# Softmax sums and V products of four heads in four 32-column tiles, with V split in even and odd values

## The chip, the cores and the metric

The kernel runs on one core of a Trainium2 chip. Its time is the device time of one execution in microseconds (us). The median of 13 runs before the change is 294.19 us, with runs from 291.63 to 298.27. One execution was profiled; it took 292.19 us, and its span from the first to the last instruction is 290.5 us. Engines are called PE (matrix multiplication), DVE (vector engine), ACT (activations), POOL (general purpose) and SP (issues most DMAs).

## The reference

Attention with forget gates, then a gated convolution FFN:

```python
scores = q @ k.T / sqrt(64)                # 8 batches, 8 heads, 576 positions, 64 values
cum = cumsum(log(clip(f, 1e-4, 1)))
attn = softmax(scores + cum[:, None] - cum[None, :], causal)
x = (attn @ v), the heads side by side     # (8, 576, 512)
h = relu(x @ w_in)                         # 1024 channels
out = (h * sigmoid(conv3(h))) @ w_out      # convolution over positions, per channel
```

The softmax's division is done after the product with V: the kernel computes the sums of the exponentials in a matmul with ones, their reciprocals, and multiplies the V product by them.

## The kernel before

**Tiling.** The 64 pairs of batch and head are worked off in 16 half batches of four heads (`hb`). A half batch consists of two steps (`i = 2*hb + p`) of two heads each (`s`). Scores are computed transposed, keys in partitions and queries along the free axis, in key blocks of 128, and only where the causal mask leaves something: the diagonal blocks (L350), the blocks off the diagonal (L341), and the last 64 positions of all four heads as a "tail" (L327). ACT takes exponentials out of PSUM (L332, L347, L357), POOL masks the diagonal blocks and the tails (L335, L360). The exponentials of a step lie in one of six tiles `pp` (off-diagonal, then masked diagonal), the tails in `pt`.

**Sums and V products.** `sweep` (L368) goes over ten pieces of queries and keys (L363). For every piece it issues one matmul for each of the two heads of the step, head `s` into the partitions `64*s` to `64*s + 63` of PSUM. With ones as weights it makes the sums (`sums`, L384), with V as weights the product (`pv`, L398). A sweep is 20 matmuls of 64 weight columns. The ones of step `c` of a batch stand in column `c` of each 32 columns (L256), so the sums of a batch's four steps are accumulated into different rows of one PSUM tile. `recip` (L389) then transposes this tile in blocks of 32 x 32 (st), and takes the reciprocals of four columns of each block (rt). `spread` (L394), once per step, spreads them over 64 partitions per head with another transpose (rb), and `norm` (L403) multiplies the V product by them and writes xt, the FFN's input. V is loaded for a whole batch and cast to fp16 by POOL, in two instructions per half batch (L231).

**FFN.** For each of eight blocks of 128 channels, `ffn1` (L410, eight matmuls) needs all four xt of the batch. ACT applies ReLU (ht, L418), DVE two steps of the convolution (u, L424 and L426), ACT the tanh (hg, L429) and DVE the gate (L433). `ffn2` (L435) multiplies by w_out; ACT evacuates (L465) and SP stores (L473).

**Order.** The kernel is written as tasks, each with its engine, an assumed duration, the tasks it comes after, the buffers it takes and gives, and a key for its priority. `Plan.play` (L36) runs through these assumed durations when the kernel is built, and fixes in which order each engine gets its instructions. On the chip, every engine works its instructions off in this order and waits where something isn't there yet. SP's and POOL's DMA issues stand in these orders as well. Buffers are rings: four PSUM tiles (ps), four of q and k (qk), six pp, four ht, three u, two each of rb, xt and hg.

**Loading q and k.** q and k arrive by transposing DMAs (L199) as 16-bit halves. In the first six half batches DVE then clears the odd rows (`clamp`, L203, four per half batch), and SP fills in rows of the cumulated gates out of an image in DRAM (`rows_of`, L218, the issues L220 and L221). Later half batches get all these rows by DMA (`fill`, L212). POOL writes the image's constants early on (L479), partly out of the q/k tile of half batch 3, whose load waits for that.

Of the kernel before, what the change touches and what calls it, by code (L numbers as in the profile page):

```python
# [9 lines left out]
FP32 = mybir.dt.float32  # L10
FP16 = mybir.dt.float16
# [103 lines left out]
def kernel(  # L115
# [11 lines left out]
    nc = tc.nc  # L127

    B, H, S, D = q.shape
    assert (B, H, S, D) == (8, 8, 576, 64)  # L130
    NKB = 5
    SL = S - 128 * (NKB - 1)
# [7 lines left out]
    HH = 4  # L140
# [3 lines left out]
    AB = 256  # L144
# [24 lines left out]
    ones_h = cpool.tile([128, 4, 64], FP16, name="ones_h")  # L169
# [5 lines left out]
    va_t = [cpool.tile([128, HH, NKB, 64], FP16, name=f"va{t}") for t in range(NVA)]  # L175
# [5 lines left out]
    rt_t = [cpool.tile([128, 18, 4], FP32, name=f"rt{t}") for t in range(2)]  # L181
# [10 lines left out]
    plan = Plan({"ps": 4, "sc": 2, "mm": 2, "pv": 2, "p": NP, "pt": NPT, "pd": 2, "p3": 2, "st": 1, "rt": 2, "rb": 2, "xt": 2, "ht": NHT,  # L192
                 "u": NU, "hg": 2, "ob": NOB, "va": NVA, "vf": NVF, "qk": RING})
    slot = plan.slot
# [36 lines left out]
    def cast_v(t_load, t_cast, hb, part, eng):  # L231
        vf, va = vf_t[slot[t_load, "vf"]][:, HH * (hb % 2):HH * (hb % 2 + 1)], va_t[slot[t_cast, "va"]]
        if part == 0:
            eng.tensor_copy(va[:, :, 0:4, :], vf[:, :, 0:4, :])  # L234
        else:
            eng.tensor_copy(va[0:SL, :, 4, :], vf[0:SL, :, 4, :])
# [16 lines left out]
    nc.gpsimd.memset(ones_h, 0.0)  # L253
    for c in range(4):
        for j in range(2):
            nc.gpsimd.memset(ones_h[:, c, 32 * j + c:32 * j + c + 1], 1.0)  # L256
# [3 lines left out]
    for t in range(NVA):  # L260
        nc.gpsimd.memset(va_t[t][64:128, :, NKB - 1, :], 0.0)
# [106 lines left out]
    def sweep(ps, i, pp, pt, left_of, first, last):  # L368

        for x, (m, q0, n, kind) in enumerate(PIECES):  # L370
            for s in range(2):
                h = (2 * i + s) % HH
                if kind == "o":
                    c = 1024 * s + OFF[m] + q0 - 128 * (m + 1)
                    p = pp[:, c:c + n]
                elif kind == "d":
                    c = 2048 + 512 * s + 128 * m
                    p = pp[:, c:c + n]
                else:
                    p = pt[:, SL * h:SL * (h + 1)]  # L380
                nc.tensor.matmul(ps[64 * s:64 * (s + 1), AB + q0:AB + q0 + n], left_of(s, h, m), p,  # L381
                                 start=first and x in (0, 3), stop=last and x in (2, 9), skip_group_check=True)

    def sums(t_first, i, t_dg, t_tail):  # L384
        c = i % 4
        sweep(ps_t[slot[t_first, "ps"]], i, pp_t[slot[t_dg, "p"]], pt_t[slot[t_tail, "pt"]],
              lambda s, h, m: ones_h[:, c, :], c == 0, c == 3)

    def recip(t_first, me):  # L389
        st, rt = st_t[0], rt_t[slot[me, "rt"]]  # L390
        nc.vector.transpose(st, ps_t[slot[t_first, "ps"]][:, AB:AB + S])
        nc.vector.reciprocal(rt, st.rearrange("p (b t) -> p b t", t=32)[:, :, 0:4])

    def spread(t_rc, me, c):  # L394
        nc.vector.transpose(rb_t[slot[me, "rb"]].rearrange("p (b t) -> p b t", t=32),  # L395
                            rt_t[slot[t_rc, "rt"]][:, :, c:c + 1].broadcast_to((128, 18, 32)))

    def pv(me, i, t_dg, t_tail, t_va):  # L398
        va = va_t[slot[t_va, "va"]]
        sweep(ps_t[slot[me, "ps"]], i, pp_t[slot[t_dg, "p"]], pt_t[slot[t_tail, "pt"]],  # L400
              lambda s, h, m: va[:, h, m, :], True, True)

    def norm(t_pv, t_rb, t_x0, c):  # L403
        nc.vector.tensor_tensor(xt_t[slot[t_x0, "xt"]][:, c, :], ps_t[slot[t_pv, "ps"]][:, AB:AB + S],  # L404
                                rb_t[slot[t_rb, "rb"]], op=ALU.mult)
# [81 lines left out]
    add = plan.add  # L487
# [21 lines left out]
    for hb in range(NHB):  # L509
# [10 lines left out]
        if hb % 2 == 0:  # L520
            t_vl[b] = add({"SP": 3.4}, [], 4 * b + 2.4, lambda me, b=b: load_v(b, me), take=["vf"], lag=3.0, dma=5.2)
        x = add({"POOL": 1.25}, [t_vl[b]], 4 * b + 3.0 + 0.4 * (hb % 2),
                lambda me, hb=hb, b=b: cast_v(t_vl[b], me, hb, 0, nc.gpsimd), take=["va"])
        y = add({"POOL": 0.5}, [t_vl[b]], 4 * b + 3.1 + 0.4 * (hb % 2),
                lambda me, hb=hb, b=b, x=x: cast_v(t_vl[b], x, hb, 1, nc.gpsimd),
                give=[("vf", t_vl[b])] if hb % 2 else [], behind=[x])
        t_va[hb] = (x, y)
# [36 lines left out]
        if hb == 1:  # L564
            t_win = weights(4, w_in_f16, moe_w_in.rearrange("(cc p) ff -> p cc ff", p=128),
                            [t_mask[1], t_mask[1], t_mask[2], t_mask[2]], 2.2, 256)
# [3 lines left out]
        if hb % 2 == 0:  # L570
            continue
        prev = None
        for c in range(4):
            i = 4 * b + c
            g = i // 2
            need = [t_mask[i], t_tmask[g], t_exp[g, i % 2, 0], t_exp[g, i % 2, 1]]
            if c == 0:
                t_s0 = prev = add({"PE": 0.75}, need + [t_mask[i + 2]], i + 3.6,
                                  lambda me, i=i, g=g: sums(me, i, t_dg[i], t_tail[g]), take=["ps"])
            else:  # L580
                prev = add({"PE": 0.75}, need, 4 * b + 3.6 + 0.1 * c,
                           lambda me, i=i, g=g, t_s0=t_s0: sums(t_s0, i, t_dg[i], t_tail[g]), behind=[prev])
        t_rc = add({"DVE": 1.5}, [prev], 4 * b + 3.5, lambda me, t_s0=t_s0: recip(t_s0, me), take=["rt"],
                   give=[("ps", t_s0)])
        for c in range(4):
            i = 4 * b + c
            g = i // 2
            last = i == 4 * b + 3
            t_rb = add({"DVE": 0.75}, [t_rc], 4 * b + 3.7 + 0.1 * c,
                       lambda me, t_rc=t_rc, c=c: spread(t_rc, me, c), take=["rb"],  # L590
                       give=[("rt", t_rc)] if last else [])
            t_pv[i] = add({"PE": 0.75}, [t_rc, *t_va[g]], 4 * b + 3.8 + 0.1 * c,
                          lambda me, i=i, g=g: pv(me, i, t_dg[i], t_tail[g], t_va[g][0]),
                          take=["ps", "pv"] + (["xt"] if c == 0 else []), behind=[t_pv[i - 1]] if c else [],
                          give=[("p", t_dg[i])] + ([("pt", t_tail[g]), ("va", t_va[g][0])] if c % 2 else []))
            t_norm[i] = add({"DVE": 0.75}, [t_pv[i], t_rb], 4 * b + 3.6 + 0.1 * c,
                            lambda me, i=i, t_rb=t_rb, b=b, c=c: norm(t_pv[i], t_rb, t_x0[b], c),
                            give=[("ps", t_pv[i]), ("pv", t_pv[i]), ("rb", t_rb)],
                            behind=[t_norm[i - 1]] if c else [])
            if c == 0:  # L600
                t_x0[b] = t_pv[i]

    for b in range(B):
        k1 = 4 * b + 5.0
        us = {}
        for ff in range(NFF):
            key = k1 + 0.5 * ff
            x = add({"PE": 1.0}, [t_norm[4 * b + c] for c in range(4)] + [t_win[ff // 2]], key,
# [86 lines left out]
```

## Time and profile before

| what | value |
|---|---|
| median of 13 runs (lowest, highest) | 294.19 us (291.63, 298.27) |
| the profiled execution, its span | 292.19 us, 290.5 us |
| PE busy | 243.1 us (84%) |
| DVE busy | 238.7 us (82%) |
| ACT busy | 197.8 us (68%) |
| POOL busy | 95.7 us (33%) |
| sums and V products (L381), matmuls | 640 and 640 |
| transposes to spread reciprocals (L395) | 32, mean 746 ns |
| products with reciprocals (L404) | 32, mean 729 ns |
| mean granted PE clock | 0.973 |

Busy time is a share of the whole span, which has a head (loads and the first scores), a stretch in which the batches follow each other with nearly the same pattern, and a tail of FFN work alone. A row of the timeline has its start, its length, the engine, the line, the operation with its tiles, and in brackets how long the engine was idle before it and what ended that. Rows can merge several equal instructions (x18). In the chain that ended last, each row is followed back from the last instruction to what released it.

### The profile page before, as it was taken

Reading aid. Unit: us, or ns where it says so; the run is one execution under the profiler, and the core shown is the slowest. Engines: PE = TensorE matmul, PEld = TensorE weight load, DVE = VectorE, ACT = ScalarE, POOL = GpSimd, SP = SyncE. Lnnn points to the kernel's source line nnn. Section 1 sums busy time; section 2 is a strip of 40 time slices with the busy share of each in tenths; the row PEclk is TensorE's granted clock in tenths of the full one; section 3 lists DMA queues with packets and bytes.
Section 4 is the critical chain, followed back from the end, with each engine's and each line's share of the span. In section 5 each row is a group of like instructions: output and inputs, shape, how many; then the busy total and the mean of one; then the engine's idle time right before and its main releaser. Section 6 shows DMA issues by size and latency. Waiting matters only on the chain.

```text
span 290.5 us, 6856 instructions
## 1 busy us (share of the span) xinstructions
PE 243.1 (84%) x2832; PEld 169.7 (58%) x2832; DVE 238.7 (82%) x322; ACT 197.8 (68%) x266; POOL 95.7 (33%) x133
## 2 busy tenths in 40 slices
PE   0099349498789799999998999999999999969990
PEld 0077237376655577567755875687568766854630
DVE  4853209989999888997997899989998999799871
ACT  1238425487665998885868878977897798526731
POOL 8626816236350326405255261126112221000000
PEclk9999958979999999999999999999999999999998
DMA  8997999999987997999999999999411001200404
GB/s 166 227 258 134 159 168 192 173 214 190 233 183 103 289 224 166 259 248 261 187 228 206 271 210 172 222 294 154 108 74 74 20 2 72 93 2 0 165 0 164
DMA packets 125683, 47.71 MB, mean 164 GB/s; under 512 B 117470, under 2 KB 120542, under 8 KB 124992
## 3 DMA queue, kind: packets, MB, share of 16 engines
q1 hardware_dynamic: 118852, 43.73, 72.4%
q0 software_dynamic: 6640, 3.25, 8.3%
q8 instruction: 22, 0.36, 0.6%
q10 hardware_dynamic: 160, 0.30, 0.4%
q14 instruction: 9, 0.07, 0.1%
HBM read 19.91 MB, written 10.58 MB: 105 GB/s over the span
## 4 chain that ended last, share of the span: by engine, by line
PE 46%; DVE 30%; ACT 8%; issue 6%; DMA 4%; POOL 3%; SPq 1%; ACTq 0%; DVEq 0%; POOLq 0%
PE ps L440 14%; PE ps L414 11%; PE ps L381 8%; PE ps L320 6%; DVE u L426 6%; DVE hg L433 6%; DVE u L424 5%; DVE xt L404 4%; DVE rb L395 3%; DMA qk<-image 3%; PE ps L454 3%; ACT pd L357 2%; ACT pp L347 2%; ACT hg L429 2%; DMA rb<-in_f_dram 2%
## 5 line engine op out<-in xcount | busy, mean ns | idle before, releaser
L320 PE MATMUL ps<-qk 128*128 128x128 bf16 (+3 forms) x576 | 63.7, 249 | 30.9 <-DVE qk L205 14.5
L414 PE MATMUL ps<-xt,w_in_f 128*128 128x288 f16 x512 | 72.2, 288 | 4.3 <-DVE xt L404 2.6
L347 ACT ACTIVATE pp<-ps 128x1024 f16<-128x1024 f32 x64 | 64.7, 1027 | 11.6 <-PE ps L320 10.4
L429 ACT ACTIVATE hg<-u,cw 128x576 f16<-128x576 f32 x64 | 49.4, 779 | 25.7 <-DVE u L426 25.4
L320 PEld LDWEIGHTS <-qk 128*128 128x128 bf16 x576 | 39.6, 102 | 43.3 <-issue 15.1
L360 POOL TENSOR_SCALAR_AFFINE_SELECT pp<-pd 128x1024 f16<-128x1024 f32 x32 | 38.5, 1202 | 73.8 <-ACT pd L357 73.5
L414 PEld LDWEIGHTS <-w_in_f 128*128 128x128 f16 x512 | 48.9, 98 | 22.4 <-issue 6.9
L426 DVE SCALAR_TENSOR_TENSOR u<-ht,cwt,u 128x576 f32<-128x576 f16 x64 | 60.8, 959 | 0.7
L433 DVE SCALAR_TENSOR_TENSOR hg<-hg,ht 128x576 f16<-128x576 f16 x64 | 53.1, 838 | 10.0 <-ACT hg L429 9.8
L424 DVE SCALAR_TENSOR_TENSOR u<-ht,cwt 128x576 f32<-128x576 f16 x64 | 55.3, 877 | 4.5 <-ACT ht L418 4.5
L440 PE MATMUL ps<-w_out_f,hg 128*128 128x512 f16 x224 | 51.5, 379 | 2.5 <-ACT pd L357 1.1
L418 ACT ACTIVATE ht<-ps 128x576 f16<-128x576 f32 x64 | 41.3, 657 | 16.4 <-PE ps L414 14.4
L440 PEld LDWEIGHTS <-hg 128*128 128x128 f16 x224 | 21.6, 98 | 26.5 <-issue 2.3
L357 ACT ACTIVATE pd<-ps 128x1024 f32<-128x1024 f32 x32 | 32.8, 1026 | 5.5 <-PE ps L325 2.4
L381 PE MATMUL ps<-pp,ones_h 128*64 128x128 f16 (+3 forms) x576 | 26.4, 243 | 1.4 <-ACT pp L347 0.8
L381 PEld LDWEIGHTS <-ones_h 128*64 128x64 f16 x640 | 23.1, 112 | 6.3 <-issue 4.6
L381 PE MATMUL ps<-pp,va 128*64 128x128 f16 (+3 forms) x576 | 24.9, 239 | 1.5 <-DVE xt L404 1.2
L335 POOL TENSOR_SCALAR_AFFINE_SELECT pt<-p 128x256 f16<-128x256 f32 x16 | 9.4, 589 | 50.0 <-ACT p L332 50.0
L234 POOL CAST va<-vf 128x1024 f16<-128x1024 f32 x16 | 18.3, 1146 | 22.1 <-DMA vf<-in_v_dram 16.1
L381 PEld LDWEIGHTS <-va 128*64 128x64 f16 x640 | 22.4, 111 | 5.6 <-issue 3.9
L395 DVE STREAM_TRANSPOSE rb<-rt 128x576 f32<-128x576 f32 x32 | 22.7, 746 | 0.0
L404 DVE TENSOR_TENSOR xt<-ps,rb 128x576 f16<-128x576 f32 x32 | 22.2, 729 | 0.0
(75 smaller groups left out, 165.8 us busy)
## 6 DMA issues: line engine op xcount, KB each, us to landing
vf<-in_v_dram SPq DMA_DIRECT2D x32, 256.0 KB, 5.9
out_dram<-ob SPq DMA_DIRECT2D x16, 512.0 KB, 2.8
qk<-blank SPq DMA_DIRECT2D x10, 540.0 KB, 5.5
vf<-in_v_dram SPq DMA_DIRECT2D x8, 128.0 KB, 5.1
w_in_f<-in_moe_w_in_dram POOLq DMA_DIRECT2D x4, 256.0 KB, 5.2
w_out_f<-in_moe_w_out_dram POOLq DMA_DIRECT2D x4, 256.0 KB, 7.1
out_dram<-ob SPq DMA_DIRECT2D x16, 64.0 KB, 3.6
blank<-qk POOLq DMA_DIRECT2D x1, 540.0 KB, 4.7
```

The lines of the kernel that those rows point to most:

```text
L320: nc.tensor.matmul(o, tk[:, h * S + k0:h * S + k0 + 128], tq[:, h * S + q0:h * S + q0 + n], start=True, stop=hb > 0)
L347: nc.scalar.activation(pp_t[slot[t_dg, "p"]][:, 1024 * s:1024 * (s + 1)], ps_t[slot[t_sc, "ps"]], AF.Exp, scale=SCALE)
L357: nc.scalar.activation(pd_t[slot[me, "pd"]], ps_t[slot[t_dg, "ps"]], AF.Exp, scale=SCALE)
L360: nc.gpsimd.affine_select(pp_t[slot[t_dg, "p"]][:, 2048:3072].rearrange("p (m j) -> p m j", j=128), pd_t[slot[t_ex, "pd"]].rearrange("p (m ...
L381: nc.tensor.matmul(ps[64 * s:64 * (s + 1), AB + q0:AB + q0 + n], left_of(s, h, m), p, start=first and x in (0, 3), stop=last and x in (2, ...
L414: nc.tensor.matmul(ps[:, MB + 288 * a:MB + 288 * (a + 1)], w_in_f16[:, cc, 128 * ff:128 * (ff + 1)], xt[:, cc, 288 * a:288 * (a + 1)], sta ...
L418: nc.scalar.activation(ht_t[slot[t_m1, "ht"]][:, 1:1 + S], ps_t[slot[t_m1, "ps"]][:, MB:MB + S], AF.Relu, scale=0.5)
L424: nc.vector.scalar_tensor_tensor(u, ht[:, 0:S], cwt[:, ff, 0:1], ht[:, 1:1 + S], op0=ALU.mult, op1=ALU.add)
L426: nc.vector.scalar_tensor_tensor(u, ht[:, 2:2 + S], cwt[:, ff, 1:2], u, op0=ALU.mult, op1=ALU.add)
L429: nc.scalar.activation(hg_t[slot[t_g0, "hg"]][:, ff, :], u_t[slot[t_u, "u"]], AF.Tanh, scale=cw[:, ff, 1:2])
L433: nc.vector.scalar_tensor_tensor(hv, hv, 1.0, ht_t[slot[t_m1, "ht"]][:, 1:1 + S], op0=ALU.add, op1=ALU.mult)
L440: nc.tensor.matmul(o, hg[:, ff, 128 * c:128 * (c + 1)], w_out_f16[:, ff, :], start=(ff == 0), stop=(ff == NFF - 1))
```

## The change

Sums and V products are made for a half batch's four heads at once. Head `h` takes the PSUM partitions `32*h` to `32*h + 31`, with 32 weight columns per matmul. A sweep is then 40 matmuls. V's 64 values don't fit 32 columns, so V is split in even and odd values when it is cast, and a half batch has one sweep of sums and two of V. The reciprocals are made per half batch: one transpose, the reciprocals of one column of each block, one transpose to spread them. Each of the two V sweeps gives one xt, in which partition `32*h + j` holds value `2*j + e` of head `h`. w_in's rows are loaded in this order, with two DMAs in place of four. The cast of V takes three POOL instructions in place of two. Sums and products no longer wait for the second half batch of a batch, and their tasks have new keys.

```diff
-    ones_h = cpool.tile([128, 4, 64], FP16, name="ones_h")
+    ones_h = cpool.tile([128, 32], FP16, name="ones_h")
...
-    va_t = [cpool.tile([128, HH, NKB, 64], FP16, name=f"va{t}") for t in range(NVA)]
+    va_t = [cpool.tile([128, HH, NKB, 2, 32], FP16, name=f"va{t}") for t in range(NVA)]
...
-    rt_t = [cpool.tile([128, 18, 4], FP32, name=f"rt{t}") for t in range(2)]
+    rt_t = [cpool.tile([128, 18, 1], FP32, name=f"rt{t}") for t in range(2)]
...
-        if part == 0:
-            eng.tensor_copy(va[:, :, 0:4, :], vf[:, :, 0:4, :])
-        else:
-            eng.tensor_copy(va[0:SL, :, 4, :], vf[0:SL, :, 4, :])
+        vf = vf.rearrange("p h m (j e) -> p h m e j", e=2)
+        if part < 2:
+            eng.tensor_copy(va[:, :, 0:4, part, :], vf[:, :, 0:4, part, :])
+        else:
+            eng.tensor_copy(va[0:SL, :, 4, :, :], vf[0:SL, :, 4, :, :])
...
-    def sweep(ps, i, pp, pt, left_of, first, last):
+    def sweep(ps, hb, t_dgs, t_tail, left_of):
+        pt = pt_t[slot[t_tail, "pt"]]
         for x, (m, q0, n, kind) in enumerate(PIECES):
-            for s in range(2):
-                h = (2 * i + s) % HH
+            for h in range(HH):
+                pp, s = pp_t[slot[t_dgs[h // 2], "p"]], h % 2
...
-                nc.tensor.matmul(ps[64 * s:64 * (s + 1), AB + q0:AB + q0 + n], left_of(s, h, m), p,
-                                 start=first and x in (0, 3), stop=last and x in (2, 9), skip_group_check=True)
+                nc.tensor.matmul(ps[32 * h:32 * (h + 1), AB + q0:AB + q0 + n], left_of(h, m), p,
+                                 start=x in (0, 3), stop=x in (2, 9), skip_group_check=True)
...
+    def recip(t_s, me):
+        st, rt, rb = st_t[0], rt_t[slot[me, "rb"]], rb_t[slot[me, "rb"]]
+        nc.vector.transpose(st, ps_t[slot[t_s, "ps"]][:, AB:AB + S])
+        nc.vector.reciprocal(rt, st.rearrange("p (b t) -> p b t", t=32)[:, :, 0:1])
+        nc.vector.transpose(rb.rearrange("p (b t) -> p b t", t=32), rt.broadcast_to((128, 18, 32)))
+
+    def pv(me, hb, e, t_dgs, t_tail, t_va):
         va = va_t[slot[t_va, "va"]]
+        sweep(ps_t[slot[me, "ps"]], hb, t_dgs, t_tail, lambda h, m: va[:, h, m, e, :])
...
         if hb == 1:
-            t_win = weights(4, w_in_f16, moe_w_in.rearrange("(cc p) ff -> p cc ff", p=128),
-                            [t_mask[1], t_mask[1], t_mask[2], t_mask[2]], 2.2, 256)
+            for x in range(2):
+                t_win.append(add({"POOL": 0.9}, [t_mask[1 + x]], 2.2 + 0.2 * x,
+                                 lambda me, x=x: nc.gpsimd.dma_start(
+                                     w_in_f16[:, 2 * x:2 * x + 2, :],
+                                     moe_w_in[256 * x:256 * (x + 1), :].rearrange("(p e) ff -> p e ff", e=2)),
+                                 lag=2.0, dma=4.5))
...
+        dgs = (t_dg[2 * hb], t_dg[2 * hb + 1])
+        need = [t_tmask[hb], t_mask[2 * hb], t_mask[2 * hb + 1]] + [t_exp[hb, p, x] for p in range(2) for x in range(2)]
+        ks = 2 * hb + (3.0 if hb % 2 else 3.0)
+        t_s = add({"PE": 0.8}, need, ks, lambda me, hb=hb, dgs=dgs: sums(me, hb, dgs, t_tail[hb]), take=["ps"])
+        t_rb = add({"DVE": 1.75}, [t_s], ks - 0.1, lambda me, t_s=t_s: recip(t_s, me), take=["rb"], give=[("ps", t_s)])
+        for e in range(2):
+            c = 4 * b + 2 * (hb % 2) + e
...
+            t_pv[c] = add({"PE": 0.8}, [t_s, *t_va[hb]], ks + 0.1 + 0.1 * e,
...
+            t_norm[c] = add({"DVE": 0.75}, [t_pv[c], t_rb], ks + 0.1 * e,
...
-            x = add({"PE": 1.0}, [t_norm[4 * b + c] for c in range(4)] + [t_win[ff // 2]], key,
+            x = add({"PE": 1.0}, [t_norm[4 * b + c] for c in range(4)] + t_win, key,
```

The orders that the planner makes change with it on every engine, in the head as well as in the repeated pattern.

## The prediction

> **What bounds the kernel now.** I read busy time by stage first. Columns: stretch, its length, then busy us and (instructions) per engine, granted clock, DMA share, GB/s.
> ```profile
> 80.82:258.96 178.14, 167.99 (x2029) 118.22 (x2028) 163.44 (x208) 139.28 (x191) 54.25 (x57) 1.00 0.79 168
> 164.81:194.09 29.28, 28.31 (x350) 20.00 (x346) 27.45 (x34) 24.25 (x34) 9.25 (x10) 1.00 1.08 228
> ```
> 80.82 and 258.96 are where the last product with the reciprocals (xt, L404) ends for batch 1 and batch 7: six batches in 178.14, 29.69 us each. In one batch PE is busy 28.31 of 29.28 us and DVE 27.45: nearly level. The chain that ended last says how they share the period (start, us, what):
> ```profile
> 188.47 2.21 PE ps L381 x60
> ...
> 193.36 0.70 DVE st L391
> 194.09 0.60 DVE rt L392
> ...
> 200.70 0.73 DVE xt L404
> ```
> PE walks from the first FFN1 of a batch (172.15 in the timeline) through 60 matmuls of sums to the last 20, which end near 193.1 (20.9 us); then DVE needs 8.1 us from st to the last xt (193.36 to 201.43), which FFN1 of the batch waits for. 20.9 + 0.3 + 8.1 = 29.3: PE and DVE in turn, in their written order, set the period. What a change frees counts only if it shortens that round trip. The tail after 258.96 is DVE's 28 convolution and gate operations. The head is another matter. PE, then SP's issues:
> ```profile
> 40.51 2.08 PE L320 MATMUL ps<-qk 128*128 128x64 bf16 x16 [8.84 <-DMA qk<-image]
> 51.35 3.35 PE L414 MATMUL ps<-xt,w_in_f 128*128 128x288 f16 x26 [0.26 <-DVE xt L404]
> 58.41 1.16 PE L320 MATMUL ps<-qk 128*128 128x64 bf16 x16 [3.71 <-DMA qk<-image]
> ```
> ```profile
> 32.48 4.24 SPq L199 DMA_TRANSPOSE qk<-in_q_dram  x1
> 36.83 0.36 SPq L220 DMA_DIRECT2D qk<-image  x1
> 37.30 0.58 SPq L221 DMA_DIRECT2D qk<-image  x1
> 37.93 2.44 SPq L199 DMA_TRANSPOSE qk<-in_k_dram  x1
> ```
> Half batch 2's scores wait 8.84 us for rows from the image (L220/L221); half batch 3's wait again, but only after 32 FFN1 matmuls of batch 0 had given DVE convolution work from 53.57 on. Below I call half batches hb0 to hb15.
>
> **Part 1, TensorE sweeps.** A sweep is 1600 columns per head. Start, us, what:
> ```profile
> 217.51 0.25 PE L320 MATMUL ps<-qk 128*128 128x192 bf16 x1
> 217.68 0.86 PE L381 MATMUL ps<-pp,ones_h 128*64 128x128 f16 x18
> ...
> 218.40 0.83 PE L381 MATMUL ps<-pp,ones_h 128*64 128x128 f16 x18
> ...
> 219.77 0.20 PE L381 MATMUL ps<-pt,ones_h 128*64 128x64 f16 x2
> 219.89 0.42 PE L414 MATMUL ps<-xt,w_in_f 128*128 128x288 f16 x2
> ```
> Two heads of 20 matmuls take 0.70 us (218.40 to 219.10), 1600 columns at 2.3 a ns: the two column tiles run beside each other. Per batch there are 8 sweeps now and 6 after (2 of sums, 4 of V, each over four heads): if four tiles run beside each other like two, -2 x 0.70 = -1.40. Against it stands the switch between full-width and column-tile matmuls: the 192 columns from 217.51 need 0.08, the sums start at 217.68, so 0.09 is lost, and 0.09 again to 219.89. In the built order a batch has 5 groups of column-tile matmuls before and 7 after: +2 x 0.2 = +0.4. Net -1.0 per batch on PE.
> The Trainium skill speaks against the four tiles: "TensorEngine Tiling (Array Packing)", Instruction Overhead, gives each matmul a floor of about 60 cycles. At the 2.4 GHz of "TensorE: Matmul & The Clock Gate" that is 25 ns, so 40 matmuls would take 1.0 us and not 0.70: +0.3 x 6 = 1.8 per batch in place of a gain. Row against it:
> ```profile
> 159.80 0.22 PE L381 MATMUL ps<-pp,ones_h 128*64 128x128 f16 x1
> 159.80 0.19 PE L381 MATMUL ps<-pt,ones_h 128*64 128x64 f16 x1
> ```
> Two matmuls in different tiles start within the same 10 ns, so the floor does not hold across tiles. I take 0.70 and keep 1.0 for the range. No run shows four tiles.
>
> **Part 2, DVE.** Before, per batch: st 0.78 + rt 0.60 + 4 spreads x 0.746 = 4.36. After, twice: st 0.78, a reciprocal of 18 elements and one spread 0.75. The reciprocal: 72 elements took 603 ns, 8 took 205 (L309), so 18 about 267. 2 x 1.80 = 3.60: -0.76 per batch. The 4 norms (729 ns each) stay.
>
> **Part 3, POOL.** The cast of 1024 elements (1.03 undisturbed) becomes two of 512 with a stride of two on the reading side. From 1024 in 1.03 and 256 in 0.39 (L236) follows 0.60 each: +0.17 per half batch; if the stride halves its speed, +1.2. POOL is 33% busy and a cast waits 16 us for V's DMA, so it lies beside; its cost is DVE slowed while POOL runs (L426 averages 959 ns where an undisturbed one takes 0.81): 0 to +0.5 per batch. The cast of the last 64 rows, the smaller memsets and the new places in va move nothing. w_in's two DMAs in place of four save about 1.5 us of POOL's issue (0.77 each) near 30 us, and FFN1's first matmul now needs both. The second is issued behind hb2's first diagonal mask, near 47, and lands 5.2 later at 52, before FFN1 can start (below): 0.
>
> **Part 4, the head, where the built order changes most.** (a) SP issues both transposes of hb3 (2.44 to 4.24 each) ahead of hb2's rows: 36.83 becomes about 40, and hb2's scores start near 43.5 instead of 40.51. (b) The V products of hb0 follow 12 of these scores; xt of hb0 ends near 48 and the last two clamps of hb3 stand behind it on DVE, so hb3's rows go out near 49.5 (before: 52.70). Landing took 5.1 then and 3.0 for hb2: 53 to 54.5. (c) Before, 32 FFN1 matmuls of batch 0 ran ahead of hb3's scores. Now all of hb3's scores precede them on PE, and on ACT all its exponentials precede the first ReLU. Seven exponentials took 6.0 us for hb1 (26.50 to 32.50), so ReLU comes at about 60.5 and the first convolution near 62 (60 to 64) instead of 53.57. Queued behind: the whole of batch 0's convolution on DVE. (d) From there DVE is fed. Before it needed 27.25 us from 53.57 to batch 1's last xt. After: -4.36 + 1.8 (hb2's reciprocals lie in the wait), and four more convolution operations of batch 0 stand ahead of that xt, +3.1: 27.8. It ends at 89.8 instead of 80.82: +9.0. The four operations are no loss: batch 7's last xt has 25 operations behind it instead of 28 or 29, so the tail is shorter by 2.4 (3.1 less 0.7 for the first convolution, which fewer leftovers cover). Head and tail: +6.6.
>
> **Part 5, the period after.** I walk the new order from the first FFN1 of a batch (0) with the steps of the trace (8 FFN1 0.98, 8 FFN2 1.73, 12 scores about 1.0, sweep 0.9 with switches, DVE operations 0.68 to 0.73). PE ends the second half's sums at 23.6. If DVE is free then, it needs 1.8 for st, rt, rb and four more operations (one gate, one convolution, two xt): FFN1 again at 28.4. But DVE comes late: it has one leftover gate (0.7) and waits for the first ReLU till 2.0, then for the second, behind an FFN2, till 4.6; it reaches the first half's st at 11.7, and the first xt of that half needs the V product at 15.6, which stands behind scores, FFN2 and FFN1: another 1.5 idle. It reaches the second st at 24.5, and FFN1 starts again at 29.2. So the period is 29.2 against 29.69: 6 x -0.49 = -2.9. Freed work turns into DVE waiting for PE inside the batch.
>
> **Sum.** +6.6 - 2.9 = +3.7 on a profiled span of 290.5, whose execution took 292.19 (1.7 around it): 295.9. That execution lay 2.0 under the median 294.19, so the median after is about 298.
>
> **Rivals.**
> (A) DVE is not late at the second st. This one ends faster. For it: an average of 0.76 freed, and ACT at 24.25 of 29.28 has room. Against: the waits of part 5. At 28.4 the six periods give -7.7, with the head -1.1: 293. It decides below 28.3, where the head's loss and 0.5% are paid: at PE's own 27.3 (28.31 - 1.0) it gives 6 x -2.4 + 6.6 = -7.7: 286.5. A smaller head loss (half: +3.3) with 28.4 gives 290. I take 290 for it.
> (B) Everything cancels: 29.0 with a head of +4: 0, 294.
> (C) Four tiles share one limit: the "gain" in sweeps becomes +1.8 per batch, most of it ahead of the second half's sums: 6 x 1.5 on the forecast, 307. That is the change not doing what it says; for it only the skill's floor, against it the common starts.
>
> **How the numbers follow.** Forecast 0.45 (295 to 301.5), A 0.28, B 0.15, C 0.12. Half a per cent is 1.5 us, about what a measurement of this kernel can tell. Faster: nearly all of A, 0.27. Within: B and the edges, 0.17. Slower: 0.56. The range for 8 in 10 runs from 287.5 (most of A) to 306 (the forecast, costlier casts, part of C).
>
> **What the profile after would show.** Part 1: 40 matmuls from start to start in 0.70, and PE busy near 236. Part 2: DVE near 233. Part 4: first u (convolution) near 62, hb2's first scores near 43.5, batch 1's last xt near 90. Part 5: 29.2 between the same xt of later batches, with DVE waiting for the V products and for ReLU. Wrong if the first convolution comes before 57, if the period is under 28.3, or if a sweep takes 1.0.

## The result and the profile after

The changed kernel takes 297.56 us (median of 11 runs, 295.92 to 301.74); the kernel before took 293.98 us as the median of 48 runs beside it. The ratio is 1.0146, with a 95% interval from 1.0113 to 1.0178: 1.5% slower. Medians here and below are of all runs, while ratios leave out runs in which the chip was disturbed, so the two can differ, most where many runs were disturbed.

The profiled execution took 298.97 us, its span is 297.2 us and its mean granted clock 0.929 (before: 292.19, 290.5, 0.973). The two profiles differ by 6.7 us where the medians differ by 3.6: the profiled execution of before lay 1.8 under its median, that of the changed kernel 1.4 above. The span is cut at the same two points as in the prediction: where the last xt (now L397) of batch 1 and of batch 7 ends.

| stretch | before | after | difference | predicted |
|---|---|---|---|---|
| head, to batch 1's last xt | 80.82 | 88.15 | +7.3 | +9.0 |
| six batches | 178.1 | 172.4 | -5.7 | -2.9 |
| tail, from batch 7's last xt | 31.6 | 36.6 | +5.0 | -2.4 |
| span | 290.5 | 297.2 | +6.7 | +3.7 |

The same stretches by window, first two of the changed kernel, then the tail of the kernel before (stretch, length, busy us and instructions of PE, weight loads, DVE, ACT, POOL, granted clock, DMA share, GB/s):

```profile
88.15:260.58 172.43, 161.33 (x2516) 109.09 (x2515) 157.55 (x207) 141.61 (x193) 62.56 (x70) 0.99 0.85 174
260.58:297.20 36.62, 27.42 (x155) 13.47 (x153) 19.51 (x27) 14.38 (x21) 0.00 (x0) 0.87 0.18 65
```
```profile
258.90:290.50 31.60, 24.76 (x154) 12.85 (x153) 22.21 (x31) 15.53 (x23) 0.00 (x0) 0.97 0.21 75
```

The repeated pattern got faster, by more than forecast. The tail got slower although DVE has fewer operations in it (27 against 31, of which 25 and 29 are convolution and gate steps): PE is busy 2.7 us longer with one instruction more, at a clock of 0.87.

**The sweeps** in the changed kernel's PE timeline (start, length, what, how many):

```profile
254.28 0.84 PE L380 MATMUL ps<-pp,va 128*32 128x128 f16 x36
254.94 0.20 PE L380 MATMUL ps<-pt,va 128*32 128x64 f16 x4
254.97 0.84 PE L380 MATMUL ps<-pp,va 128*32 128x128 f16 x36
```

From start to start 40 matmuls take 0.69 us. The four tiles run beside each other as two did. Of DVE's groups the new reciprocal, and of POOL's the cast (busy, mean ns, idle before and releaser):

```profile
L235 POOL CAST va<-vf 128x512 f16<-128x512 f32 x32 | 23.0, 740 | 15.3 <-PE ps L380 9.5 <-DMA vf<-in_v_dram 5.8
L389 DVE RECIPROCAL rt<-st 128x18 f32<-128x18 f32 x16 | 4.3, 267 | 0.5
```

**The head**: three of PE's rows in the changed kernel, then the first convolution on DVE:

```profile
43.19 1.23 PE L318 MATMUL ps<-qk 128*128 128x64 bf16 x12 [7.58 <-DMA qk<-image]
...
53.58 1.23 PE L318 MATMUL ps<-qk 128*128 128x64 bf16 x12 [2.61 <-issue]
...
59.22 4.08 PE L407 MATMUL ps<-xt,w_in_f 128*128 128x288 f16 x32
```
```profile
62.56 0.82 DVE L417 SCALAR_TENSOR_TENSOR u<-ht,cwt 128x576 f32<-128x576 f16 x1 [2.91 <-issue]
```

hb2's scores begin at 43.19 (before: 40.51), hb3's at 53.58 (58.41), but all of batch 0's FFN1 stands behind them, and the first convolution begins at 62.56 instead of 53.57.

**A settled period**, 204.79 to 232.76, where the last xt of two batches end:

```profile
204.79:232.76 27.97, 27.18 (x426) 18.39 (x424) 25.16 (x35) 24.27 (x34) 7.55 (x8) 1.00 0.45 109
```

PE 27.18 of 27.97 us and DVE 25.16; the period in the trace of before was 29.3, with 28.3 and 27.45. Over the six batches the mean is 28.7, because the first (batch 1 to 2) takes 32.0 and the other five 28.1. The six of before are uneven too. From last xt to last xt, batch 1 to batch 7:

| | 1 to 2 | 2 to 3 | 3 to 4 | 4 to 5 | 5 to 6 | 6 to 7 |
|---|---|---|---|---|---|---|
| before | 32.2 | 27.3 | 31.9 | 29.3 | 29.3 | 28.2 |
| after | 32.0 | 28.1 | 28.3 | 28.1 | 28.0 | 27.8 |

So 3.6 of the 5.7 us gained come from one period, 3 to 4, and 0.9 are lost in the one ahead of it.

**The tail**, PE's rows and then DVE's, and last PE's of the kernel before:

```profile
255.77 0.66 PE L407 MATMUL ps<-xt,w_in_f 128*128 128x288 f16 x4
259.97 1.30 PE L407 MATMUL ps<-xt,w_in_f 128*128 128x288 f16 x4 [3.54 <-DVE xt L397]
261.07 9.13 PE L433 MATMUL ps<-w_out_f,hg 128*128 128x512 f16 x32
270.14 1.06 PE L438 MATMUL ps<-w_out_f,hg 128*64 128x256 f16 x16
271.13 4.09 PE L407 MATMUL ps<-xt,w_in_f 128*128 128x288 f16 x32
```
```profile
264.57 0.76 DVE L426 SCALAR_TENSOR_TENSOR hg<-hg,ht 128x576 f16<-128x576 f16 x1 [0.84 <-ACT hg L422]
273.01 0.82 DVE L417 SCALAR_TENSOR_TENSOR u<-ht,cwt 128x576 f32<-128x576 f16 x1 [7.68 <-ACT ht L411]
```
```profile
258.29 0.41 PE L414 MATMUL ps<-xt,w_in_f 128*128 128x288 f16 x2 [1.58 <-DVE xt L404]
258.96 3.35 PE L414 MATMUL ps<-xt,w_in_f 128*128 128x288 f16 x26 [0.26 <-DVE xt L404]
262.14 7.07 PE L440 MATMUL ps<-w_out_f,hg 128*128 128x512 f16 x32
```

Only one FFN1 block (8 matmuls) of batch 7 stands ahead of batch 6's 48 FFN2 matmuls; before it was four. DVE gates the one block that it has at 264.57 and then has nothing for 7.68 us, with seven of eight blocks of the last batch still to come. And the 32 FFN2 matmuls take 9.13 us, where they took 7.07 before.

### The profile page after: what moved, and what is told of

Same layout as the page of the kernel before. It is cut to its first block, busy times and chain, and to the rows that moved or that the text cites. A ratio compares the mean times of both kernels' runs of the same rounds, so it can differ in the third digit from the quotient of the medians.

```text
span 297.2 us, 8134 instructions
## 1 busy us (share of the span) xinstructions
PE 240.6 (81%) x3472; PEld 161.1 (54%) x3472; DVE 230.3 (77%) x322; ACT 199.3 (67%) x266; POOL 103.4 (35%) x139
## 4 chain that ended last, share of the span: by engine, by line
DVE 42%; PE 40%; ACT 6%; issue 5%; SPq 2%; DMA 2%; POOL 1%; ACTq 0%; DVEq 0%; POOLq 0%
PE ps L433 14%; DVE u L419 11%; DVE u L417 11%; PE ps L407 10%; DVE hg L426 8%; PE ps L318 7%; PE ps L380 5%; DVE xt L397 3%; DVE rb L390 2%; DVE st L388 2%; SPq L199 2%; ACT pp L345 2%; ACT ht L411 2%; DMA rb<-in_f_dram 1%; PE ps L321 1%
## 5 line engine op out<-in xcount | busy, mean ns | idle before, releaser
L318 PE MATMUL ps<-qk 128*128 128x128 bf16 (+3 forms) x576 | 66.3, 251 | 33.9 <-DVE qk L205 14.2
L417 DVE SCALAR_TENSOR_TENSOR u<-ht,cwt 128x576 f32<-128x576 f16 x64 | 55.5, 873 | 22.5 <-ACT ht L411 19.5
L318 PEld LDWEIGHTS <-qk 128*128 128x128 bf16 x576 | 39.7, 102 | 49.5 <-issue 24.0
L407 PEld LDWEIGHTS <-w_in_f 128*128 128x128 f16 x512 | 49.1, 98 | 28.1 <-issue 12.3
L433 PE MATMUL ps<-w_out_f,hg 128*128 128x512 f16 x224 | 54.9, 391 | 0.1
L426 DVE SCALAR_TENSOR_TENSOR hg<-hg,ht 128x576 f16<-128x576 f16 x64 | 50.1, 785 | 1.8 <-ACT hg L422 1.5
L333 POOL TENSOR_SCALAR_AFFINE_SELECT pt<-p 128x256 f16<-128x256 f32 x16 | 11.6, 726 | 76.1 <-ACT p L330 76.1
L380 PE MATMUL ps<-pp,va 128*32 128x128 f16 (+3 forms) x1152 | 29.1, 254 | 1.2 <-ACT ht L411 0.9
L380 PEld LDWEIGHTS <-va 128*32 128x32 f16 x1280 | 23.8, 104 | 8.3 <-issue 5.2
L235 POOL CAST va<-vf 128x512 f16<-128x512 f32 x32 | 23.0, 740 | 15.3 <-PE ps L380 9.5
L397 DVE TENSOR_TENSOR xt<-ps,rb 128x576 f16<-128x576 f32 x32 | 23.5, 752 | 6.1 <-PE ps L380 5.6
L458 ACT COPY ob<-ps 128x1024 f32<-128x1024 f32 (+1 forms) x23 | 18.0, 787 | 9.0 <-PE ps L433 7.0
L388 DVE STREAM_TRANSPOSE st<-ps 128x576 f32<-128x576 f32 x16 | 12.4, 773 | 10.8 <-PE ps L380 10.7
L380 PE MATMUL ps<-pp,ones_h 128*32 128x128 f16 (+3 forms) x576 | 15.5, 251 | 2.9 <-ACT pp L345 2.9
```

What stands on the lines that cost most here:

```text
L318: nc.tensor.matmul(o, tk[:, h * S + k0:h * S + k0 + 128], tq[:, h * S + q0:h * S + q0 + n], start=True, stop=hb > 0)
L380: nc.tensor.matmul(ps[32 * h:32 * (h + 1), AB + q0:AB + q0 + n], left_of(h, m), p, start=x in (0, 3), stop=x in (2, 9), skip_group_check=True)
L407: nc.tensor.matmul(ps[:, MB + 288 * a:MB + 288 * (a + 1)], w_in_f16[:, cc, 128 * ff:128 * (ff + 1)], xt[:, cc, 288 * a:288 * (a + 1)], sta ...
L417: nc.vector.scalar_tensor_tensor(u, ht[:, 0:S], cwt[:, ff, 0:1], ht[:, 1:1 + S], op0=ALU.mult, op1=ALU.add)
L426: nc.vector.scalar_tensor_tensor(hv, hv, 1.0, ht_t[slot[t_m1, "ht"]][:, 1:1 + S], op0=ALU.add, op1=ALU.mult)
L433: nc.tensor.matmul(o, hg[:, ff, 128 * c:128 * (c + 1)], w_out_f16[:, ff, :], start=(ff == 0), stop=(ff == NFF - 1))
```

## The experiments

The first four runs shared one chip and one set of runs of the kernel before (median 295.38 us), the next four another (296.39), e9_rows_hb3 a third (295.49) and the last two a fourth (295.43). Ratios are to the kernel before on the same chip; 1.0146 of the changed kernel, which was not run again beside them, is the number to hold them against.

**Was it the order in the tail?** One key: the FFN2 of batch 6 later in the planner's order, so that four FFN1 blocks of batch 7 precede it, as before the change.

```diff
-            key = k1 + 4.0 + (0.8 if b < B - 2 else 0.1) * c
+            key = k1 + (4.0 if b < B - 2 else 5.6) + (0.8 if b < B - 2 else 0.1) * c
```

> The changed kernel with one key: batch 6's FFN2 gets a later one, so that four FFN1 blocks of batch 7 stand ahead of it on PE, as in the kernel before (one in the changed kernel). Theory (the tail is longer because DVE starves for 7.7 us behind 32 FFN2 matmuls): DVE's wait goes, the stretch from batch 7's last xt to the end falls from 36.6 to about 31, time 5 to 6 below the changed kernel, about 292. Rival (DVE's wait is only PE's FFN2 work moved, the same work has to be done anyway and the end is PE's): within 1.5 of 297.6.

296.28 us, ratio 1.003 (0.9993 to 1.0067): 1.2% or 3.4 us taken from the changed kernel, less than the 5 to 6 expected. The tail of the profiled run is 34.3 us: 2.3 of the 5.0 are gone, the other 2.7 are not. The order was one half of it. (Batch 1's last xt ends at 86.09 in this profile, 2.1 us earlier than in the changed kernel's, though the order in the head is the same. A difference of that size between two heads need not come from an edit.) The other half stands in PE's rows of this run:

```profile
253.66 0.66 PE L407 MATMUL ps<-xt,w_in_f 128*128 128x288 f16 x4
257.86 6.40 PE L407 MATMUL ps<-xt,w_in_f 128*128 128x288 f16 x28 [3.54 <-DVE xt L397]
264.10 7.07 PE L433 MATMUL ps<-w_out_f,hg 128*128 128x512 f16 x32
```

28 FFN1 matmuls take 6.40 us, where 32 take 4.09 above. The clock is what differs (stretch and length first, granted clock third from the end):

```profile
256.60:263.50 6.90, 5.61 (x24) 3.31 (x24) 4.99 (x7) 2.50 (x4) 0.00 (x0) 0.51 0.00 0
```

**Was it the wait for w_in?** In the planner, FFN1 no longer waits for the w_in DMAs.

```diff
-            x = add({"PE": 1.0}, [t_norm[4 * b + c] for c in range(4)] + t_win, key,
+            x = add({"PE": 1.0}, [t_norm[4 * b + c] for c in range(4)], key,
```

> The changed kernel, where FFN1's tasks don't name w_in's DMAs among what they come after, so the planner orders them as if w_in were there (the chip still waits for the data). Theory (the two DMAs, all of FFN1 behind both, are what made the planner put half batch 3's scores and all its exponentials ahead of batch 0's FFN1): first convolution near 53 instead of 62.6, batch 1's last xt near 82 instead of 88.15, time 4 to 7 lower, about 292. Rival 1 (w_in does land late: PE then stands in FFN1 with half batch 3's scores behind it): first convolution after 57, gain under 2. Rival 2 (the head's wait is covered later): first convolution early, time within 1.5 of 297.6.

300.83 us, ratio 1.0184 (1.0113 to 1.0255): not faster. The first convolution came at 53.57, as in the kernel before, and batch 1's last xt at 84.7, 3.4 earlier than in the changed kernel and not 9. In between PE stood still for rows of hb4:

```profile
76.66 0.37 PE L318 MATMUL ps<-qk 128*128 128x64 bf16 x4 [8.59 <-DMA qk<-image]
```

But that wait is not where the other 5.6 us went, since DVE had work all the while. From the first convolution to batch 1's last xt, in the kernel before, the changed kernel and this run (DVE's busy time and instructions are the third pair):

```profile
53.57:80.82 27.25, 20.43 (x280) 15.55 (x278) 25.85 (x35) 19.84 (x26) 10.38 (x10) 0.94 1.21 203
62.56:88.15 25.59, 17.08 (x275) 12.09 (x273) 25.48 (x35) 14.65 (x21) 9.30 (x10) 0.73 1.11 162
53.57:84.70 31.13, 19.77 (x357) 14.51 (x356) 30.96 (x41) 19.65 (x27) 11.90 (x13) 0.84 1.14 172
```

DVE is busy for 30.96 of 31.13 us. The order puts 41 instructions into the stretch instead of 35 (hb2's reciprocals and three more clamps), 5.5 us more of work. Two later periods (29.5 and 31.8) gave up the rest; the tail (35.8) is about that of the changed kernel.

**Both together.** The two edits above in one kernel.

> Both edits of the two runs before. Theory: they lie in different stretches and add: 10 to 12 below the changed kernel, about 286.5, that is 2.5% faster than the kernel before, since the period of 28.0 to 28.7 stays. Rival (one of the two only moves waiting into the other stretch): not more than the larger of the two, about 292.

300.88 us, ratio 1.0077 (1.0032 to 1.0123). The two do not add up: it is better than e2_win and no better than e1_tail.

**The wait alone, in the kernel before.** There, each FFN1 block waits only for its own part of w_in; here it waits for all four DMAs, as in the changed kernel.

```diff
-            x = add({"PE": 1.0}, [t_norm[4 * b + c] for c in range(4)] + [t_win[ff // 2]], key,
+            x = add({"PE": 1.0}, [t_norm[4 * b + c] for c in range(4)] + t_win, key,
```

> The kernel before with that one wait alone: every FFN1 task comes after all of w_in's four DMAs. Sums, products, reciprocals and casts as before. Theory (the wait moves the order in the head, without any of the four-tile work): scores and exponentials of half batch 3 go ahead of FFN1, first convolution between 55 and 59 instead of 53.6, time 2 to 5 higher. Rival (the head's order comes from the half batch tasks): order and time as before, within 1.5 of 294.

296.96 us, ratio 1.008 (1.0045 to 1.0115): 2.4 us slower. The first convolution moved from 53.57 to 61.91, more than expected, and batch 1's last xt from 80.82 to 84.76, by 3.9. The later periods take 1.5 us less in all, the tail 1.7 more (more on that tail at the end). So this one line of the diff, by what it does to the planned order, costs about half of the head's 7.3 us, and an 8 us later first convolution costs 4, not 8, since fewer of DVE's instructions (29) are left to stand behind it:

```profile
61.91:84.76 22.85, 18.73 (x272) 14.31 (x271) 22.66 (x29) 17.83 (x24) 11.33 (x11) 1.00 1.08 188
```

**The half clock.** As e1_tail, and in the last half batch the reciprocals and the two xt get a key 3.0 lower, which puts them ahead of three convolution and gate steps on DVE.

```diff
         ks = 2 * hb + (3.0 if hb % 2 else 3.0)
+        kr = ks - (3.0 if hb == NHB - 1 else 0.0)
...
-        t_rb = add({"DVE": 1.75}, [t_s], ks - 0.1,
+        t_rb = add({"DVE": 1.75}, [t_s], kr - 0.1,
...
-            t_norm[c] = add({"DVE": 0.75}, [t_pv[c], t_rb], ks + 0.1 * e,
+            t_norm[c] = add({"DVE": 0.75}, [t_pv[c], t_rb], kr + 0.1 * e,
```

> Batch 6's FFN2 keyed as in e1_tail, and in the last half batch the reciprocal (st, rt, rb) and its two xt are put ahead of three conv and gate steps on DVE; nothing is left out. Theory: what was left of the tail's loss in e1_tail (34.3 against 31.6 us before) is a half clock that follows TensorE's 3.54 us wait for the last xt, under which 28 FFN1 matmuls took 6.40 us where they take 3.6. With the chain earlier on DVE the last xt should end about 2 us sooner (256.3 instead of 258.47), the wait fall to about 1.8 us, no half clock follow, and the FFN2 of batch 6 begin at about 260 instead of 264.1: tail about 31.5 counted from the same xt, time 4 lower than e1_tail: 291 to 293 us. Rival: the half clock comes without regard to this wait: then 28 FFN1 still take about 6.4, and the time falls by 1.5 to 2 only (294 to 295).

290.95 us, ratio 0.9897 (0.981 to 0.9984). PE's rows:

```profile
257.65 0.41 PE L407 MATMUL ps<-xt,w_in_f 128*128 128x288 f16 x2 [1.33 <-DVE xt L397]
258.31 3.35 PE L407 MATMUL ps<-xt,w_in_f 128*128 128x288 f16 x26 [0.26 <-DVE xt L397]
261.50 7.07 PE L433 MATMUL ps<-w_out_f,hg 128*128 128x512 f16 x32
```

The waits are 1.33 and 0.26 us instead of 3.54, the clock stays at full speed, 26 matmuls take 3.35. The tail is 31.9 us, that of the kernel before (31.6). Counted from batch 6's last xt to the end, which leaves the head out, e1_tail needs 62.1 us and this run 57.5: 4.6 us, where the theory said 4. The rival (half clock without regard to the wait) falls.

> The kernel of e5_tail_rec once more, beside the kernel before and e10_rows_hb4 in the same rounds, since its 4 runs left an interval of 0.981 to 0.998. Theory: it keeps the 2.5 us that the tail's two changes are worth beyond the kernel before: ratio 0.985 to 0.995, 290 to 293 us. Rival: those 4 runs were a lucky few: ratio 0.995 to 1.005.

291.48 us, ratio 0.9884 (0.9833 to 0.9935). It holds: with two keys set, the changed kernel is 1.2% faster than the one before.

**Which engine sets the period?** Once the 40 sums are issued twice per half batch (0.69 us of PE), once the transpose that spreads the reciprocals (0.8 us of DVE).

```diff
-        sweep(ps_t[slot[me, "ps"]], hb, t_dgs, t_tail, lambda h, m: ones_h)
+        for _ in range(2):
+            sweep(ps_t[slot[me, "ps"]], hb, t_dgs, t_tail, lambda h, m: ones_h)
```

> The changed kernel, with each half batch's 40 matmuls of the sums issued twice into the same tiles (the second starts them afresh, so the values are the same). Theory: TensorE sets the settled period now (27.18 of 27.97 us): 0.69 more per half batch gives 1.4 more per period (29.3 to 29.5 in the last five), 7 to 9 more in all: 304.5 to 306.5 us. Rival: the period is set by the chain through DVE (sums, reciprocal, xt): 0.7 longer once per half batch in it and hidden otherwise: periods 28.0 to 28.6, 0 to 4 more, 297.5 to 301.

```diff
-        nc.vector.transpose(rb.rearrange("p (b t) -> p b t", t=32), rt.broadcast_to((128, 18, 32)))
+        for _ in range(2):
+            nc.vector.transpose(rb.rearrange("p (b t) -> p b t", t=32), rt.broadcast_to((128, 18, 32)))
```

> The changed kernel, with the transpose that spreads the reciprocals (rb) issued twice per half batch, 0.72 us of DVE each. Theory (TensorE sets the period, DVE waits 2.5 us in it): 1.44 more DVE per period goes into those waits: periods 28.0 to 28.4, 0 to 3 more in all, plus 0.7 in the tail: 298 to 301 us. Rival (DVE or the chain through it sets the period): 29.4 per period and 8 to 10 more in all: 305 to 308.

Sums twice: 304.54 us, ratio 1.0327 (1.0173 to 1.0482). Spread twice: 308.0 us, ratio 1.0487 (1.0362 to 1.0612). A settled period of each, sums first:

```profile
210.99:239.66 28.67, 28.50 (x507) 19.68 (x505) 25.14 (x36) 24.45 (x34) 7.53 (x8) 1.00 0.21 64
```
```profile
211.00:240.67 29.67, 27.19 (x425) 18.38 (x423) 27.18 (x37) 24.27 (x34) 6.93 (x6) 0.99 0.20 62
```

The sums added 1.3 us of PE and 0.7 to the period: PE's 0.8 us of idle time (27.97 - 27.18) shrank to 0.2. The time fell into the theory's range, but the settled period, 28.67, is nearer to the rival's 28.0 to 28.6 than to the theory's 29.3 to 29.5; two earlier periods took 30.6 and 30.5. The spreads added about 2.0 us of DVE's busy time (1.6 by the two operations, the rest by a convolution step that took longer) and 1.7 to the period, although DVE had 2.8 us of idle time in it. So the forecast of e8_spread_twice, that DVE's waits would swallow it, was wrong, and its rival (29.4 per period, 305 to 308 us) came. Its DVE rows say why: all the waits that remain in this batch are at its start (the lines of this kernel lie one further down, so that L418 is L417 above).

```profile
212.88 0.82 DVE L418 SCALAR_TENSOR_TENSOR u<-ht,cwt 128x576 f32<-128x576 f16 x1 [1.22 <-ACT ht L412]
...
215.02 0.82 DVE L418 SCALAR_TENSOR_TENSOR u<-ht,cwt 128x576 f32<-128x576 f16 x1 [0.47 <-ACT ht L412]
...
217.73 0.82 DVE L418 SCALAR_TENSOR_TENSOR u<-ht,cwt 128x576 f32<-128x576 f16 x1 [0.49 <-ACT ht L412]
```

There DVE waits for FFN1 and ReLU of the new batch, 2.2 us in all, and an operation added later can't use that. From 217.73 to the last xt (ending at 240.67) it never waits, and PE waits for it instead:

```profile
210.39 1.14 PE L408 MATMUL ps<-xt,w_in_f 128*128 128x288 f16 x8 [1.62 <-DVE xt L398]
...
240.06 1.84 PE L408 MATMUL ps<-xt,w_in_f 128*128 128x288 f16 x8 [1.89 <-DVE xt L398]
```

Both engines set the period of the changed kernel: PE with under 0.8 us to spare, DVE with under 0.5 (in the changed kernel's DVE rows, two waits of 0.28 and 0.18 for the V product and for ReLU are all that it has after the start).

**Can the head be won back?** Three steps, each on top of the tail's two edits. First (e6_rows_tail) hb2's clamps are keyed earlier and FFN1's wait for w_in becomes an order behind its DMAs, without their assumed duration.

```diff
-                    cl.append(add({"DVE": 0.6}, [t_ld[hb, s]], base - 1.0 + 0.1 * (2 * p + s),
+                    cl.append(add({"DVE": 0.6}, [t_ld[hb, s]], base - (1.6 if hb == 2 else 1.0) + 0.1 * (2 * p + s),
...
-            x = add({"PE": 1.0}, [t_norm[4 * b + c] for c in range(4)] + t_win, key,
-                    lambda me, b=b, ff=ff: ffn1(me, t_x0[b], ff), take=["ps", "mm", "ht"],
+            x = add({"PE": 1.0}, [t_norm[4 * b + c] for c in range(4)], key,
+                    lambda me, b=b, ff=ff: ffn1(me, t_x0[b], ff), take=["ps", "mm", "ht"], behind=t_win,
```

> As e5_tail_rec, and in the head the clamps of hb2 are keyed 0.6 earlier and batch 0's FFN1 has no wait for w_in in the planner's model beyond standing behind its DMAs; nothing is left out. Theory: the head's loss is SP's order (hb3's k transpose of 5.83 us ahead of hb2's rows) and the late first convolution. Rows of hb2 should go out at about 35 instead of 40.7, the first convolution start at 54 to 57 instead of 62.6, batch 1's last xt end at 82 to 85 instead of 88.15: 3 to 5 lower than e5_tail_rec, 287 to 290 us, faster than the kernel before. Rival: as in e2_win, what is won at the first convolution is given back by a wait for hb4's rows and by later periods: batch 1's xt gains under 3 us, periods of batches 3 to 5 grow to 29 to 32, and the time is that of e5_tail_rec or above it.

292.32 us, ratio 0.9912 (0.9885 to 0.994). hb2's rows went out at 37.60 (expected 35) and the first convolution began at 56.50, as expected; batch 1's last xt at 87.08, only 1.1 earlier than in the changed kernel. The rival is what happened: nothing gained on e5_tail_rec (0.9897). The first period fell to 29.5 us, but that of batch 4 to 5 grew to 32.1. Next, hb3's clamps come earlier as well.

```diff
-                    cl.append(add({"DVE": 0.6}, [t_ld[hb, s]], base - (1.6 if hb == 2 else 1.0) + 0.1 * (2 * p + s),
+                    cl.append(add({"DVE": 0.6}, [t_ld[hb, s]], base - (1.6 if hb in (2, 3) else 1.0) + 0.1 * (2 * p + s),
```

> As e6_rows_tail, with hb3's four clamps keyed 0.6 earlier too, so that all four stand ahead of the first convolution on DVE (in e6_rows_tail the last stood behind it, went at 57.24 us, and SP's queue, V's load of batch 2 and hb4's transposes waited for it until 57.84); nothing is left out. Theory: SP's queue is what gives the head's gain back. hb3's rows go out at 54 instead of 57.84, hb4's at 66 to 67 instead of 70.6, and batch 1's last xt ends at 83 to 85 instead of 87.08: time 2 to 3 lower than e6_rows_tail, 289 to 290.5 us. Rival: batch 1's last xt follows from the 25 to 30 us of DVE's work behind the first convolution, whose start doesn't move: xt at 86 to 88, time 291.5 to 293.

297.14 us, ratio 1.0006 (0.9967 to 1.0044). The rows went out at 53.87 as planned, hb4's at 67.89 and 71.66, and batch 1's last xt ended at 87.17. The theory (SP's queue at hb3) falls, and the time is worse than the rival said. Why it is worse stays open: the profiled run, the fastest of 22, has a span of 290.2 us, e6_rows_tail's has 290.0. Last, from e6_rows_tail, hb4's transposes and clamps come earlier.

```diff
-                t_ld[hb, s] = add({"SP": 2.4}, old, base - 2.2 + 0.1 * s,
+                t_ld[hb, s] = add({"SP": 2.4}, old, base - (4.0 if hb == 4 else 2.2) + 0.1 * s,
...
-                    cl.append(add({"DVE": 0.6}, [t_ld[hb, s]], base - (1.6 if hb == 2 else 1.0) + 0.1 * (2 * p + s),
+                    cl.append(add({"DVE": 0.6}, [t_ld[hb, s]], base - (1.6 if hb == 2 else 2.2 if hb == 4 else 1.0) + 0.1 * (2 * p + s),
```

> As e6_rows_tail, with hb4's transposes and its four clamps keyed 1.2 to 1.8 earlier, so that they stand four to seven DVE operations further ahead; nothing is left out. Theory: what is left of the head's loss is hb4's rows, which went out at 64.93 to 65.40 us in the kernel before and at 69.4 to 75.3 in every version of the changed one; with them at 64 to 66, TensorE's waits between 63 and 77 us fall from about 6 to under 4 and batch 1's last xt ends at 83 to 85 instead of 87.08: time 289 to 290.5 us, 2 to 3 lower than e6_rows_tail. Rival: batch 1's xt follows from ScalarE (exponentials and relu, which TensorE waits for at 63 to 78 us) and from DVE's work behind the first convolution: then it ends at 86 to 88 as before this step, and the time is within 1 us of e6_rows_tail or above it.

290.56 us, ratio 0.9863 (0.9817 to 0.991), the best of all, though not apart from e11_tail_rec_again within the intervals. SP's rows of it and, second, of the changed kernel, for the rows of hb4:

```profile
62.21 0.25 SPq L220 DMA_DIRECT2D qk<-image  x1
63.47 0.60 SPq L221 DMA_DIRECT2D qk<-image  x1
```
```profile
72.12 0.38 SPq L220 DMA_DIRECT2D qk<-image  x1
75.32 0.61 SPq L221 DMA_DIRECT2D qk<-image  x1
```

Batch 1's last xt ends at 85.28 (e6_rows_tail: 87.08; e11_tail_rec_again, on the same chip: 87.79), just outside the expected 83 to 85. That hb4's rows did this is not shown. DVE's stretch from the first convolution to that xt, e6_rows_tail and then this run:

```profile
56.50:87.08 30.58, 24.29 (x330) 16.71 (x329) 29.30 (x38) 20.91 (x28) 12.59 (x12) 0.75 1.05 171
55.23:85.28 30.05, 20.58 (x331) 14.61 (x330) 28.76 (x38) 20.81 (x28) 10.16 (x12) 0.93 1.02 178
```

Of the 1.8 us, 1.3 are there when the first convolution begins, ahead of hb4's rows, and only 0.5 lie in the stretch that these rows could shorten. Both are within what heads of one and the same order differ by: batch 1's last xt ends at 88.15, 86.09, 88.05 and 87.79 in the changed kernel, e1_tail, e5_tail_rec and e11_tail_rec_again. To the kernel before (80.82) 4.5 us are left: the first convolution comes 1.7 later, and DVE's stretch behind it is 2.8 longer, with 38 instructions in place of 35.

## Why the prediction was right, and where it was not

The time (298.0 said, 297.56 measured) and the sign were right. The terms were not all, and the closeness of the number is luck in two ways. Against the profile the head was 1.7 us too high, the six batches 2.8 too high and the tail 7.4 too low, which in part cancels: +3.7 was said for the span, +6.7 measured. And the medians, for which 298 was said, differ by only 3.6 us.

- **Part 1** (sweeps): right. 0.69 us for 40 matmuls, said 0.70; PE busy 240.6, said near 236 (matmuls at half clock in the head and the tail are in it). Rival C falls. The floor of 60 cycles per matmul that the Trainium skill states ("TensorEngine Tiling (Array Packing)", Instruction Overhead) does not hold for matmuls that alternate between four tiles: it would have been 1.0 us for the 40; measured are 17 ns per matmul.
- **Part 2** (DVE): right. The reciprocal took 267 ns, said "about 267"; DVE busy 230.3, said near 233.
- **Part 3** (POOL): the cast takes 740 ns on the mean and 621 at least, said 0.60 undisturbed, so the stride did not halve its speed; POOL is 35% busy. Nothing waits for it in the settled batches.
- **Part 4** (head): right in its mechanism, high by 1.7. Rows of hb2 at 40.66 (said about 40), scores 43.19 (43.5), hb3's rows 48.96 (49.5), first convolution 62.56 (62), last xt 88.15 (89.8). DVE was fed from the first convolution on (25.48 of 25.59 us busy), as said; its stretch was put at 27.8 us. In one point the reasoning was short: it put w_in at 0 because the DMA lands before FFN1 "can start". It lands in time, but its place in the planner is what moves FFN1 behind hb3's scores; e4_before_win prices this at 3.9 us of the head.
- **Part 5** (period): mis-sized, in two ways. The walk gave 29.2 for a settled batch but was held against the mean 29.69, where settled batches took 29.3. The -2.9 was thus mostly the uneven periods, of which the walk says nothing; one of them (31.9 to 28.3) made most of the measured -5.7. And settled batches take 28.0, not 29.2. Counted from FFN1's start at 204.18, the second sums end at 22.9 instead of 23.6, and st begins at 24.0 instead of 24.5: DVE is late there, as said, by 1.1 us. The 1.5 us that it was to wait for the first half's V product were 0.28. And "four more operations" did not all have to end before FFN1: it starts (232.15) 0.6 us before the last xt ends. By the prediction's own mark (under 28.3) its walk was wrong. The period is rival A's, but A's reason ("DVE is not late at the second st") did not come true. e7_sums_twice and e8_spread_twice show a tie of PE and DVE, so neither engine alone has more to give.
- **The tail**: the step that failed, "batch 7's last xt has 25 operations behind it instead of 28 or 29, so the tail is shorter by 2.4". The count was right (25 convolution and gate steps against 29), but operations are not what the tail is made of when they have no input. It took 5.0 more. e1_tail shows 2.3 of it to be the order (one FFN1 block ahead of batch 6's FFN2 instead of four, DVE idle for 7.68 us), and e5_tail_rec the rest: PE waits 3.54 us for the last xt, whose reciprocals stand behind convolution steps on DVE, and then runs at half clock for 7 us. The order could have been read beforehand in the built order of instructions; the half clock was harder to foresee: the trace of before has it in its head, around PE's waits of 8.84 and 3.71 us, but near its tail only waits of 0.26, 1.58 and 0.26 us.

That rival A's period came and its sign did not is the tail's doing: without it (e5_tail_rec, e11_tail_rec_again) the same kernel ends at 291 us, with the whole head loss still in it. That this is near the 290 taken for A is chance, as A put the head's loss at half.

## What to carry to other kernels

Cost the ends of a pipeline by the order of instructions as built, not by counting what is left: here a planner's keys, tuned for the old pattern, turned a gain of 1.2% into a loss of 1.5%. When a period is made of two engines in turn, idle time counts as spare only if it lies after the point where the new work would stand; DVE had 2.8 us idle per batch and could not take 1.6 more. After an edit that lets an engine run ahead, look for the first long wait that it opens on PE, since the clock can stay low long after the wait is over (5.3 us in the changed kernel's tail). And before a wait of one engine is blamed for a late tile, look whether the engine that makes the tile was busy all the while, as DVE was in e2_win.

## What was not expected of the hardware

- In the changed kernel's tail PE's clock was halved from 258.4 us, 2.0 us into its wait of 3.54, and stayed so for 6.8 us, of which 5.3 were work (in e1_tail it was 2.3 us into the same wait). After waits of 1.33 and 0.26 us (e5_tail_rec) it stayed at 1.00.
- In all thirteen traces, the stretches of full and of half clock that the trace records whole last multiples of 3.41 us (3.4, 6.8, 10.2 and so on). So these runs read as if the clock were set once per window of 3.41 us, by how much of the window PE was idle, and not by the length of a single wait. Two such windows each in the tail of the changed kernel, of the kernel before and of e4_before_win (PE's busy time behind the length, the clock third from the end):

```profile
255.00:258.41 3.41, 1.44 (x58) 1.04 (x45) 3.34 (x6) 0.77 (x1) 0.00 (x0) 1.00 0.18 43
258.42:261.83 3.41, 1.83 (x6) 0.80 (x6) 2.83 (x5) 1.23 (x2) 0.00 (x0) 0.50 0.00 0
```
```profile
254.28:257.69 3.41, 2.05 (x40) 1.52 (x35) 3.41 (x7) 0.00 (x0) 0.00 (x0) 1.00 0.00 0
257.69:261.10 3.41, 2.55 (x20) 1.91 (x20) 3.38 (x5) 1.44 (x3) 0.00 (x0) 1.00 0.00 0
```
```profile
258.48:261.89 3.41, 1.33 (x9) 0.79 (x9) 3.41 (x6) 0.00 (x0) 0.00 (x0) 1.00 0.00 0
261.90:265.30 3.40, 3.40 (x17) 2.10 (x15) 3.37 (x6) 2.63 (x4) 0.00 (x0) 0.50 0.00 0
```

- The last two kernels have the same waits there, 0.26, 1.58 and 0.26 us. In the kernel before two windows share them (1.36 and 0.86 us idle) and the clock stays; in e4_before_win one window holds all of them (2.08 us), the clock falls, 26 FFN1 matmuls take 5.02 us instead of 3.35, and the tail 33.3 instead of 31.6. So part of a difference between two tails can be where the windows happen to lie. In the thirteen traces the clock fell after every window with over 2.0 us of idle time and after none with under 1.7; between these it went either way. The two waits of e5_tail_rec, 1.6 us in all, stay under that wherever a window begins.
- In e8_spread_twice the same eight FFN1 matmuls took 1.14 us after a wait of 1.62, but 1.84 after one of 1.89, with half clock from 240.3 to 243.7: a window's end divides the first wait, while the second lies in one window. The Trainium skill ("TensorE: Matmul & The Clock Gate", Part 1) gives an idle window of about 3.4 us before the clock falls. The length agrees with the windows here; but about 2 us of idle time in one of them were enough.
- Four 32-column tiles of different heads overlapped as well as two wider ones: 40 matmuls in 0.69 us, 17 ns each, against 35 ns each for 20 in two 64-column tiles.
